# A third matrix product for 17 steps in place of a VectorE sum, and four gathers spread over four steps, in a Fourier-mixing and gated-convolution kernel

## The chip, the cores and the metric

The kernel runs on one core of a Trainium2 chip. The metric is the device time of one execution in microseconds (us). A core has five engines with a queue of instructions each: TensorE (in the profile PE, and PEld for its weight loads), VectorE (DVE), ScalarE (ACT), GpSimd (POOL) and SyncE (SP), which here only issues transfers. Each engine works its queue in the order in which the program issues; between engines there are semaphores. SBUF is the working memory, PSUM the memory that TensorE writes its products to.

## The reference

Per batch (8), a sequence of 3136 rows with 256 features is transformed by a two-dimensional Fourier transform, of which the real part is kept. Then follow a matrix product to 1024 features, a ReLU, a convolution with three taps along the sequence (one weight per tap and feature), a gate (the value times its sigmoid) and a matrix product back to 256 features. All numbers are float32.

```python
X = np.fft.fft(np.fft.fft(x, axis=1), axis=2).real
h = np.maximum(X @ w_in, 0.0)
conv_out = sum(conv_w[k] * hp[:, k:k + S, :] for k in range(3))   # hp: h with a zero row on both ends
out = (h * sigmoid(conv_out)) @ w_out
```

## The kernel before, in words

**The transform.** For each batch, x is loaded in two halves: one plain transfer by SP and four gathers by indirect DMA on GpSimd (`mirrored`, L131), which bring rows in mirrored order. VectorE folds the halves by sums and differences (`fold_ops`, L151 to L194; 14 operations per batch), TensorE multiplies the folded rows by tables of cosines and sines (`units`, tile `pd`), and VectorE combines these into two tiles per batch, `pt` and `qt` (`PQ`), of 128 features by 1569 frequencies. The transform along the features is merged into the weight: `G` holds two products of `w_in` with cosines and sines. One feature of the spectrum is handled apart (`Feature`, tile `ft`), and arrives as a row `eb`.

**The steps.** The main part works in 256 steps (batch, chunk, feature block): 8 batches, 4 chunks of the frequencies (some 386 columns each), 8 blocks of 128 of the 1024 features. Because x is real, the frequencies k and S-k come from the same two products: with `pa` = seed + G0 pt and `pb` = G1 qt, row k of h is relu(pa + pb), row S-k is relu(pa - pb). So one step makes a front half and a back half of a row tile `h` of 770 or 832 columns.

The code issues everything by hand, in the order of a loop over turns t (`LAG` is 3), in which each engine's queue receives:

- ScalarE: the sigmoids of step t-2 (L725, two instructions); the two copies of `pb` of step t+1 into `nb`, as pb and as -pb (`copies`, L693); the seed of step t+2 into `pa` (`seed`, L672: feature row times weight); the first tap of step t (`first_tap`, L707); at the end of a chunk six copies of finished outputs (L752).
- TensorE: the two products of step t+1 (`products`: `pb`, then `pa`); then `mm2` of step t-3 (12 instructions into `po`, accumulated over the eight feature blocks); then parts of the transform of the next batch.
- VectorE: the two sums of step t (`combine`, L702: `TENSOR_ADD_SAT` adds `pa` and one half of `nb`, clips below at 0 and writes a half of `h`, the back half in reverse order); the second tap of step t-1 (L712); a fold, or part of the conversion of the weights from 64-bit floats (L543 to L561, in turns 0, 2, 3, 5 and 7); the third tap of step t-1 (L712); the gate of step t-2 for its first 385 columns or so (L733).
- GpSimd: in chunk 0 a small memset of the two end columns of `h` (`row_of`, L678, called at the head of `combine`); the gate of step t-2 for the other columns (L732, L735); the gathers.

The lists of extra work are filled by `at(turn, where, fn)`: "first" stands behind the sigmoids, "act" behind the copies, "dve" between the taps, "pool" and "load" behind the gate, "pe" at the end. For batch 1, folds stand in turns 9 to 19 (the first half of x in turns 9 to 13, the second from turn 14 on), the products of its transform from turn 20 on. `feat.place` (POOL, VectorE, ACT) stands in turn 5, its stages in turns 14 to 18.

Buffers: `pa` has two, `pb` one, `nb` two, `h` four, `g` five. Waits between engines are derived from which instruction reads and writes which tile.

Of the kernel before, what the change touches and what calls it, by code (L numbers as in the profile page):

```python
# [12 lines left out]
AF = mybir.ActivationFunctionType  # L13
# [19 lines left out]
BIG = 3.4028234663852886e38  # L33
# [3 lines left out]
def kernel(  # L37
# [10 lines left out]
    nc = tc.nc  # L48
    B, S, D = x.shape
    F = moe_w_in.shape[1]  # L50
    P = 128
# [9 lines left out]
    NF = F // P  # L61
# [27 lines left out]
    act = nc.scalar.activation  # L89

    def mm(o, l, r, start, stop):
        nc.tensor.matmul(o, l, r, start=start, stop=stop, skip_group_check=True)  # L92
# [16 lines left out]
    def load_ops(b, h, eng, other=None, held=False):  # L109


        def plain():
            t = xp.tile([P, 8, 2, D], F32, name="xh", tag="xh")
            xh[b, h] = t
            if held:

                nc.gpsimd.memset(t[0:1, 0, 0, 0:1], 0.0)
            eng.dma_start(out=t[0:NP, 0:4], in_=bass.AP(
                tensor=x.tensor, offset=x.offset + (b * S + 1 + 2 * h) * D,
                ap=[[HQ * D, NP], [Q4 * D, 4], [1, 2 * D]]))  # L120

        def zero():
            t = xh[b, h]
            for s0, n, r in ((0, 4, 0), (4, 3, 1), (7, 1, 0)):
                (other or eng).dma_start(out=t[NP:KR, s0:s0 + n], in_=bass.AP(
                    tensor=x.tensor, offset=x.offset + (b * S + r * Q4) * D,
                    ap=[[D, 1], [Q4 * D, n], [0, 2], [1, D]]))

        def mirrored(m):
            def f():  # L130
                nc.gpsimd.indirect_dma_start(  # L131
                    out=xh[b, h][0:NP, 7 - m].rearrange("p q d -> p (q d)"),
                    out_offset=None,
                    in_=bass.AP(tensor=x.tensor, offset=x.offset,
                                ap=[[2 * D, B * S // 2], [1, 2 * D]]),
                    in_offset=bass.IndirectOffsetOnAxis(ap=idx[0:NP, 0:1], axis=0),
                    element_offset=(b * S + (4 - m) * Q4 - HO + 2 * (1 - h)) * D)
            return f
        return [plain] + [zero] * h + [mirrored(m) for m in range(4)]
# [73 lines left out]
    PQ, eb, er = {}, {}, {}  # L213
# [416 lines left out]
    G = const.tile([P, 2, F], F32, name="G")  # L630
# [29 lines left out]
    hs, gs, pa, pb, po, nb = {}, {}, {}, {}, {}, {}  # L660

    def cut(s):
        b, c, f = s
        ch = chunks[c]
        return ch, ch.k1 - ch.k0, slice(f * P, (f + 1) * P)

    def seed(s):
# [3 lines left out]
        pa[s] = psa.tile([P, 512], F32, name="pa", tag="pa")  # L671
        act(pa[s][:, 0:n], eb[b, c], AF.Copy, scale=ge[:, f:f + 1])  # L672

    def row_of(s):
        hs[s] = hp.tile([P, HW], F32, name="h", tag="h")
        w = chunks[s[1]].w
        if chunks[s[1]].zeros:
            nc.gpsimd.memset(hs[s][:, 0:w:w - 1], 0.0)  # L678

    def products(s):  # L680
        b, c, f = s
        ch, n, fs = cut(s)
        pb[s] = psb.tile([P, 512], F32, name="pb", tag="pb")
        mm(pb[s][:, 0:n], G[0:P - 1, 1, fs], PQ[b][1][0:P - 1, ch.k0:ch.k1], True, True)
        mm(pa[s][:, 0:n], G[:, 0, fs], PQ[b][0][:, ch.k0:ch.k1], False, True)

    def copies(s):

        ch, n, fs = cut(s)
        p = pb.pop(s)  # L690
        nb[s] = nbp.tile([P, 2, HN], F32, name="nb", tag="nb")
        for i, cols in enumerate((ch.fcols, ch.cols)):
            act(nb[s][:, i, cols], p[:, cols], AF.Copy, scale=-1.0 if i else 1.0)  # L693

    def combine(s):

        ch, n, fs = cut(s)
        a, c = pa.pop(s), nb.pop(s)
        row_of(s)
        h = hs[s]  # L700
        for i, (to, cols) in enumerate(((h[:, ch.front], ch.fcols), (h[:, ch.back][:, ::-1], ch.cols))):
            nc.vector._custom_dve(TENSOR_ADD_SAT, out=to, in0=a[:, cols], in1=c[:, i, cols], s0=BIG, s1=0.0)  # L702

    def first_tap(s):
        n = chunks[s[1]].w - 2
# [99 lines left out]
    n = chunks[0].k1  # L805
    p = psd.tile([P, 512], F32, name="pd", tag="pd")
# [12 lines left out]
    def at(cycle, where, fn):  # L819
        side.setdefault((cycle, where), []).append(fn)  # L820
# [11 lines left out]
    for cycle, c in ((2, 0), (3, 2), (5, 4), (7, 6)):  # L832
        shared(cycle, w_out, c)
    for j, fn in enumerate(load_ops(1, 1, nc.sync)):
        at(NF + 1 + j // 3, "load", fn)

# [22 lines left out]
    for b in range(1, B):  # L861
        begin, us, *_ = units(b)
        us = us[0:4] + us[5:]
        c0, n = ends[b], per * b - 3 - ends[b]
# [12 lines left out]
    for b in range(1, B):  # L877
        ops, singles = fold_ops(b)
        c0, n = ends[b - 1], ends[b] - ends[b - 1]
# [14 lines left out]
    n = len(steps)  # L894
    seed(steps[0])
    seed(steps[1])
    products(steps[0])
    copies(steps[0])
    column(1)
    for t in range(n + LAG):  # L900
        def run(where):
            for fn in side.get((t, where), []):
                fn()
        if 0 <= t - 2 < n:
            sigmoid(steps[t - 2])
        run("first")
        if t + 1 < n:
            products(steps[t + 1])
            copies(steps[t + 1])
        run("act")  # L910
        if t < n:
            combine(steps[t])
        if t + 2 < n:
            seed(steps[t + 2])
        if t < n:
            first_tap(steps[t])

        if 0 <= t - 1 < n:
            tap(steps[t - 1], 1)
        run("dve")  # L920
        if 0 <= t - 1 < n:
            tap(steps[t - 1], 2)
        if 0 <= t - 2 < n:
            gate(steps[t - 2])
        run("pool")
        run("load")
        if t >= LAG:
            mm2(steps[t - LAG])
        run("pe")
# [66 lines left out]
```

## Time and profile before

| | |
|---|---|
| median of 10 runs | 1196.52 us (1193.44 to 1198.23) |
| the profiled execution | 1195.56 us |
| its span, first to last instruction | 1193.6 us |
| TensorE busy | 1156.1 us, 97% of the span, 4802 matmuls |
| VectorE busy | 1134.5 us, 95% |
| ScalarE busy | 879.0 us, 74% |
| GpSimd busy | 476.8 us, 40% |
| mean granted TensorE clock | 0.996 of full speed |

The busy time of an engine is the sum of its instructions' times; a busy time per window, a timeline of one engine and a list of what ended each idle time are taken from the same execution. A row of a timeline gives the start in us from the span's start, the length, the engine, the line of the kernel, the operation, what it writes and reads, and how many instructions are merged (x2); the rows of merged instructions overlap the next by a little, so the distance from one start to the next is what an instruction costs its queue. A clock of 1.00 is full speed.

Turn 0 begins at about 46 us. The table of steps that the prediction uses, by the start of VectorE's sums (L702): step 3 at 62.22, step 6 at 78.63, step 10 at 97.10, step 12 at 105.97, step 13 at 113.39, step 20 at 148.05 us.

### The profile page before, as it was taken

How to read it: one execution, taken by the hardware profiler on the slowest of the kernel's cores; microseconds unless marked ns; L12 is line 12 of the kernel's file. 1: busy time of each engine (PE TensorE's matmuls, PEld its weight loads, DVE VectorE, ACT ScalarE, POOL GpSimd, SP SyncE). 2: the span in 40 equal slices, each digit the busy share in tenths (PEclk: the TensorE clock that was granted, in tenths of full speed). 3: DMA queues.
4: the chain of work that ended last, by engine and by line, in shares of the span. 5: the costliest groups of instructions: out<-in, count | busy, mean ns of one | idle time of the engine just before them, and what ended most of it. 6: DMA issues, size and time to landing. Idle time of an engine off the chain costs nothing.

```text
span 1193.6 us, 15307 instructions
## 1 busy us (share of the span) xinstructions
PE 1156.1 (97%) x4802; PEld 889.1 (74%) x4802; DVE 1134.5 (95%) x1642; ACT 879.0 (74%) x1824; POOL 476.8 (40%) x540
## 2 busy tenths in 40 slices
PE   4978999999999999999999999999999999999998
PEld 2756677678777777777777777777777777777776
DVE  7899999999999999999999999999998998999996
ACT  2577667677777777777777777787776777788884
POOL 5225636454273333624345243632224232442224
PEclk9999999999999999999999999999999999999999
DMA  9802243212031210202021020310001100110000
GB/s 226 193 18 81 72 57 101 62 54 71 10 95 45 68 41 24 85 27 81 27 88 52 20 62 27 96 40 27 27 23 32 32 27 27 47 34 28 27 27 31
DMA packets 70067, 66.07 MB, mean 55 GB/s; under 512 B 28107, under 2 KB 57683, under 8 KB 69987
## 3 DMA queue, kind: packets, MB, share of 16 engines
q1 hardware_dynamic: 64349, 51.98, 15.4%
q0 software_dynamic: 5120, 12.85, 3.9%
q8 instruction: 38, 0.62, 0.2%
q14 instruction: 42, 0.34, 0.1%
q10 hardware_dynamic: 518, 0.28, 0.1%
HBM read 39.33 MB, written 25.74 MB: 55 GB/s over the span
## 4 chain that ended last, share of the span: by engine, by line
PE 87%; DVE 4%; issue 3%; POOL 3%; ACT 2%; DMA 0%; ACTq 0%; POOLq 0%; DVEq 0%; SPq 0%
PE po L92 53%; PE pb L92 14%; PE pa L92 13%; PE pd L92 7%; DVE g L712 2%; POOL xh L131 1%; DVE h L702 1%; ACT nb L693 0%; ACT os L752 0%; DVE g L733 0%; ACT g L725 0%; POOL left L735 0%; POOL g L732 0%; ACT pa L672 0%; DMA er<-qt 0%
## 5 line engine op out<-in xcount | busy, mean ns | idle before, releaser
L92 PE MATMUL po<-wout,g 128*128 128x256 f32 x3072 | 708.4, 380 | 15.7 <-DVE g L733 15.5
L92 PEld LDWEIGHTS po<-wout,g 128*128 128x128 f32 x3072 | 581.6, 190 | 162.9 <-DVE g L733 29.2
L712 DVE SCALAR_TENSOR_TENSOR g<-h,cw,g 128x770 f32<-128x770 f32 (+1 forms) x512 | 580.3, 1133 | 6.2 <-ACT g L707 2.2
L732 POOL TENSOR_TENSOR g<-g,h 128x385 f32<-128x385 f32 (+1 forms) x256 | 276.1, 1079 | 670.3 <-ACT g L725 468.3
L693 ACT ACTIVATE nb<-pb 128x386 f32<-128x386 f32 (+3 forms) x512 | 227.5, 498 | 183.7 <-PE pb L92 183.1
L725 ACT ACTIVATE g<-g 128x385 f32<-128x385 f32 (+2 forms) x512 | 244.4, 529 | 81.8 <-DVE g L712 78.5
L702 DVE CUSTOM_DVE_ANT_0 h<-pa,nb 128x386 f32<-128x386 f32 (+3 forms) x512 | 264.2, 556 | 6.5 <-POOL h L678 6.5
L707 ACT ACTIVATE g<-h,cw 128x770 f32<-128x770 f32 (+1 forms) x256 | 244.0, 953 | 0.0
L92 PE MATMUL pb<-qt,G 127*128 127x387 f32 (+2 forms) x512 | 213.8, 498 | 0.9 <-ACT G L641 0.9
L92 PE MATMUL pa<-pt,G 128*128 128x387 f32 (+2 forms) x512 | 211.8, 494 | 0.0
L672 ACT ACTIVATE pa<-eb,ge 128x387 f32<-128x387 f32 (+2 forms) x256 | 154.3, 603 | 2.5 <-DVE h L702 1.9
L92 PEld LDWEIGHTS pa<-pt,G 128*128 128x128 f32 x512 | 97.0, 189 | 73.5 <-issue 18.8
L733 DVE TENSOR_TENSOR g<-g,h 128x385 f32<-128x385 f32 (+1 forms) x256 | 147.5, 576 | 2.2 <-ACT g L725 2.2
L92 PE MATMUL pd<-tab,w 98*128 98x196 f32 (+3 forms) x448 | 118.4, 356 | 0.0
L131 POOL DMA_INDIRECT xh<-in_x_dram,idx x64 | 105.7, 1651 | 13.3 <-issue 10.6
L92 PEld LDWEIGHTS pb<-qt,G 127*128 127x128 f32 x512 | 91.0, 190 | 19.0 <-ACT G L641 1.8
L92 PEld LDWEIGHTS pd<-tab,w 98*128 98x128 f32 (+1 forms) x448 | 83.7, 191 | 12.3
L735 POOL TENSOR_TENSOR left<-g,h 128x64 f32<-128x64 f32 x64 | 63.8, 997 | 0.0
L752 ACT COPY os<-po 128x256 f32<-128x256 f32 x196 | 57.7, 392 | 8.1 <-PE po L92 4.7
L156 DVE TENSOR_TENSOR xh<-xh 98x1020 f32<-98x1020 f32 (+1 forms) x32 | 39.4, 1237 | 3.2 <-DMA xh<-in_x_dram,idx 3.2
L167 DVE TENSOR_TENSOR xh<-xh 98x1024 f32<-98x1024 f32 (+1 forms) x32 | 38.9, 1217 | 0.1
L178 POOL COPY w<-xh 98x4 f32<-98x4 f32 (+1 forms) x32 | 21.2, 662 | 7.3 <-DVE xh L172 3.7
(120 smaller groups left out, 315.3 us busy)
## 6 DMA issues: line engine op xcount, KB each, us to landing
out_dram<-os SPq DMA_DIRECT2D x192, 128.0 KB
xh<-in_x_dram SPq DMA_DIRECT2D x16, 784.0 KB
eb<-ed SPq DMA_DIRECT2D x16, 193.5 KB
tab<-dft_seq_dram SPq DMA_DIRECT2D x4, 589.5 KB
raw<-in_moe_w_in_dram SPq DMA_DIRECT2D x4, 512.0 KB
raw<-in_moe_w_out_dram SPq DMA_DIRECT2D x1, 2048.0 KB
eb<-ed SPq DMA_DIRECT2D x8, 209.0 KB
eb<-ed SPq DMA_DIRECT2D x7, 193.0 KB
```

Of the source, the lines that this page charges most:

```text
L92: nc.tensor.matmul(o, l, r, start=start, stop=stop, skip_group_check=True)
L131: nc.gpsimd.indirect_dma_start(out=xh[b, h][0:NP, 7 - m].rearrange("p q d -> p (q d)"), out_offset=None, in_=bass.AP(tensor=x.tensor, offs ...
L672: act(pa[s][:, 0:n], eb[b, c], AF.Copy, scale=ge[:, f:f + 1])
L693: act(nb[s][:, i, cols], p[:, cols], AF.Copy, scale=-1.0 if i else 1.0)
L702: nc.vector._custom_dve(TENSOR_ADD_SAT, out=to, in0=a[:, cols], in1=c[:, i, cols], s0=BIG, s1=0.0)
L707: act(gs[s], hs[s][:, 0:n], AF.Copy, scale=cw[:, 0, s[2]:s[2] + 1])
L712: stt(out=g, in0=h[:, k:k + n], scalar=cw[:, k, f:f + 1], in1=g, op0=ALU.mult, op1=ALU.add)
L725: act(gs[s][:, c], gs[s][:, c], AF.Sigmoid)
L732: gt(g[:, p], g[:, p], h[:, p], op=ALU.mult)
L733: vt(g[:, v], g[:, v], h[:, v], op=ALU.mult)
L735: gt(left[:, f, b % 2 * LEFT:(b % 2 + 1) * LEFT], g[:, r], h[:, r], op=ALU.mult)
L752: nc.scalar.copy(out=osb[:, j % 2], in_=pt[:, j % 2])
```

## The change

In steps 3 to 19 of batch 0 (`triple`), TensorE adds the `pb` product once more, into `pa`, so that `pa` becomes pa + pb. The front half of `h` is then made by ScalarE, as a Relu of `pa`; VectorE makes the back half alone, from `pa` - 2 pb, for which the single remaining copy of `pb` carries the factor -2. For these steps `row_of` is called in `copies`, one turn earlier than before. In all other steps nothing changes.

Of the six operations that load the second half of x of batch 1, the plain load, the zero rows and the first gather stay in turn 9; the other three gathers, which stood in turn 10 together, stand in turns 10, 11 and 12.

```diff
+    def triple(s):
+
+        return s[0] == 0 and 3 <= s[1] * NF + s[2] < 20
+
...
-        mm(pa[s][:, 0:n], G[:, 0, fs], PQ[b][0][:, ch.k0:ch.k1], False, True)
+        mm(pa[s][:, 0:n], G[:, 0, fs], PQ[b][0][:, ch.k0:ch.k1], False, not triple(s))
+        if triple(s):
+            mm(pa[s][:, 0:n], G[0:P - 1, 1, fs], PQ[b][1][0:P - 1, ch.k0:ch.k1], False, True)
...
-        for i, cols in enumerate((ch.fcols, ch.cols)):
-            act(nb[s][:, i, cols], p[:, cols], AF.Copy, scale=-1.0 if i else 1.0)
+        if triple(s):
+            act(nb[s][:, 1, ch.cols], p[:, ch.cols], AF.Copy, scale=-2.0)
+            row_of(s)
+            act(hs[s][:, ch.front], pa[s][:, ch.fcols], AF.Relu)
+        else:
+            for i, cols in enumerate((ch.fcols, ch.cols)):
+                act(nb[s][:, i, cols], p[:, cols], AF.Copy, scale=-1.0 if i else 1.0)
...
-        row_of(s)
+        if not triple(s):
+            row_of(s)
         h = hs[s]
         for i, (to, cols) in enumerate(((h[:, ch.front], ch.fcols), (h[:, ch.back][:, ::-1], ch.cols))):
-            nc.vector._custom_dve(TENSOR_ADD_SAT, out=to, in0=a[:, cols], in1=c[:, i, cols], s0=BIG, s1=0.0)
+            if i or not triple(s):
+                nc.vector._custom_dve(TENSOR_ADD_SAT, out=to, in0=a[:, cols], in1=c[:, i, cols],
+                                      s0=BIG, s1=0.0)
...
     for j, fn in enumerate(load_ops(1, 1, nc.sync)):
-        at(NF + 1 + j // 3, "load", fn)
+        at(NF + 1 + max(j - 2, 0), "load", fn)
```

## The prediction

> **What bounds the kernel now.** A step is one (batch, chunk, feature block), 256 in all; "turn t" is the pass of the step loop that adds up step t. TensorE's products of step t run in turn t-1, its output matmuls (`mm2`) of step t in turn t+3. I first read the page's busy line, which says only that two engines are near full:
>
> ```profile
> PE 1156.1 (97%) x4802; PEld 889.1 (74%) x4802; DVE 1134.5 (95%) x1642; ACT 879.0 (74%) x1824; POOL 476.8 (40%) x540
> ```
>
> So I read the table of busy times by stage next (columns: window, its length, then busy us of PE, PEld, DVE, ACT, POOL, granted clock, DMA share, GB/s). The change acts in turns 2 to 19, about 62 to 148 us; the third row is the stage behind it, the last one the steady state:
>
> ```profile
> 62.00:97.00 35.00, 28.59 (x112) 20.86 (x112) 33.49 (x54) 23.12 (x46) 8.98 (x19) 1.00 0.13 35
> 97.00:148.00 51.00, 45.14 (x174) 31.94 (x174) 50.93 (x72) 36.73 (x94) 30.59 (x23) 0.97 0.25 76
> 148.00:200.00 52.00, 51.82 (x223) 40.43 (x224) 51.19 (x80) 34.42 (x70) 24.75 (x27) 1.00 0.44 83
> 330.00:700.00 370.00, 370.00 (x1551) 289.03 (x1550) 359.85 (x524) 284.37 (x585) 157.70 (x176) 1.00 0.19 57
> ```
>
> Up to 148 us VectorE is full (33.49 of 35, 50.93 of 51) and TensorE is not; from 148 on TensorE is. The timelines show how the one waits for the other. VectorE in turn 10 (start, length; the number in brackets elsewhere is idle time):
>
> ```profile
> 97.10 1.02 DVE L702 CUSTOM_DVE_ANT_0 h<-pa,nb 128x386 f32<-128x386 f32 x2
> 98.04 1.01 DVE L712 SCALAR_TENSOR_TENSOR g<-h,cw,g 128x770 f32<-128x770 f32 x1
> 98.97 1.22 DVE L167 TENSOR_TENSOR xh<-xh 98x1024 f32<-98x1024 f32 x1
> 100.10 1.02 DVE L712 SCALAR_TENSOR_TENSOR g<-h,cw,g 128x770 f32<-128x770 f32 x1
> 101.03 0.55 DVE L733 TENSOR_TENSOR g<-g,h 128x385 f32<-128x385 f32 x1
> ```
>
> The two sums, the taps with a fold between them, the gate: each starts as the one before it ends. TensorE, four of the lines of the same stretch:
>
> ```profile
> 94.74 0.81 PE L92 MATMUL pb<-qt,G 127*128 127x387 f32 x2
> 95.40 0.81 PE L92 MATMUL pa<-pt,G 128*128 128x387 f32 x2
> 97.24 2.86 PE L92 MATMUL po<-wout,g 128*128 128x256 f32 x12 [1.03 <-DVE g L733]
> ...
> 113.53 4.46 PE L92 MATMUL po<-wout,g 128*128 128x256 f32 x12 [2.81 <-DVE g L733]
> ```
>
> `mm2` waits for the gate; behind the 2.81 us of idleness the clock row for 113.5 to 117.8 grants 0.61, and the block takes 4.30 us to the next product instead of 2.59. That too lies under VectorE now. The chain of waits says the same: between 60 and 113 us it runs mainly over DVE lines.
>
> **What the change takes off VectorE.** In 17 steps (3 to 19) one of two sums goes. From the first L702 (97.10) to the tap behind the pair (98.04) is 0.94 us, so one sum is 0.47: 17 x 0.47 = 8.0 us. VectorE's turns 3 to 19 run from 62.22 to 148.05, 85.8 us. One stall in them also goes: in turn 6 the sum waited 1.20 us for the memset of L678, queued on POOL behind `feat.place`; that memset is now issued one turn earlier, ahead of it. (Now step 7's memset stands behind `feat.place`: done at about 77.2, it holds the Relu of step 7, whose product ends at 76.3, for 0.9 us, on ScalarE, where the margin worked out below is 3.6.) Left: 85.8 - 8.0 - 1.2 = 76.6 us.
>
> **What it puts on TensorE.** The third product repeats the `pb` product into `pa`: by the starts above (94.74 to 95.40) it costs 0.655 us; bounds are this and 0.81, its own row, if it could not overlap its neighbour. Before: from `mm2` of step 0 (62.02) to that of step 17 (148.18) are 86.2 us. In them lie 17 blocks of `mm2` (2.59), 17 pairs of products (1.31) and the feature stage (2.0): 44.0 + 22.3 + 2.0 = 68.3, so 17.9 us are idle or slowed. The third products of steps 5 to 19 fall in here: 15 x 0.655 = 9.8. Those of steps 3 and 4 run before 62.02, 1.3 us, of which 0.7 fall in the gap from 61.33 to 62.02; 0.6 stay. TensorE without any idle time: 68.3 + 9.8 + 0.6 = 78.7 us. That exceeds VectorE's 76.6: **the bound passes to TensorE**, and the stage can shrink by 86.2 - 78.7 = 7.5 us at most.
>
> **Does it reach that?** I walked both queues through. TensorE would start `mm2` of step k at 62.64 + 4.56k; VectorE ends turn k+2, with the gate of step k, at 67.4, 70.7, 76.0, 79.3, 84.5, 87.4, 92.6, 96.5 for k = 1 to 8. TensorE comes to these at 67.2, 71.8, 76.3, 80.9, 85.4, 90.0, 94.6, 99.1. Only k = 1 (0.2 late) and k = 3 (nearly) make it wait: 0.3 us. Later the margin is 2 us and more, enough for the 1.7 us by which the tap at 106.90 was drawn out to 2.71 beside two POOL gates. In the steady state TensorE is busy 370.00 of 370 us beside a VectorE at 359.85, so a TensorE without gaps beside a nearly full VectorE exists in this kernel.
>
> **ScalarE: an instruction exchanged, a wait added.** The second copy of `pb` (two copies take 0.75 us of queue, one 0.37) becomes a Relu of `pa` of the same width: 0.37 to 0.55 (a sigmoid's row is 0.47); I take no change. L545 runs Relu between sigmoids without a table load, so none is added. But the Relu waits for the third product, 1.31 us behind `pb`, where the copy waited for `pb` alone: ScalarE stands up to 1.31 - 0.37 = 0.94 us. Behind it queue the seed of step t+2 (wanted by TensorE 2.59 + 0.65 us later; it takes 0.5) and the first tap of step t (wanted by VectorE in turn t+1). ScalarE idles 35.0 - 23.1 = 11.9 and 51.0 - 36.7 = 14.3 us here, 1.5 a turn, which covers it. From the third product over Relu, seed and first tap (2.0), tap to gate (3.5) and a further turn (4.6) to `mm2` are 10.1 us; TensorE asks for it after three turns, 13.7. Margin 3.6. The Relu also needs the `h` buffer (four of them) that the gate three steps back frees, on VectorE and on POOL.
>
> [...]
>
> **Gathers.** Turn 10 issues three gathers on POOL at once:
>
> ```profile
> 98.41 1.52 POOL L131 DMA_INDIRECT xh<-in_x_dram,idx  x1 [0.19 <-issue]
> 100.23 2.20 POOL L131 DMA_INDIRECT xh<-in_x_dram,idx  x1 [0.30 <-issue]
> 102.74 4.15 POOL L131 DMA_INDIRECT xh<-in_x_dram,idx  x1 [0.30 <-ACT nb L693]
> 106.92 0.88 POOL L732 TENSOR_TENSOR g<-g,h 128x385 f32<-128x385 f32 x1
> ```
>
> The gate at 106.92 could have run at about 102 (its sigmoid ends at 102.2). Now it would hold the Relu of step 13 through the `h` buffer, and `mm2`; one gather a turn (1.5 to 4.2 us against a turn of 4.56) lets each gate through. Nothing is late: the last is issued in turn 12, lands some 4 us later (median of `xh`) and is read in turn 15. SP's load is not moved. By itself this is worth 0 (TensorE waited 0.18 for it) to 1.7 us (the drawn-out tap); as TensorE is the bound after, I count 0.
>
> **Sum.** 7.5 - 0.3, less 0.5 for POOL hand-offs like the one above: 6.7 us (bounds: with 0.81 for the third product 17 x 0.155 = 2.6 less, 4.1; nothing lost, 7.5). Behind 148 us TensorE has no gap to 200 (51.82 of 52), so the earlier start is passed on. VectorE's own lead is not: at 187.88 it waits for ScalarE even now. The profiled execution, 1195.56 (span 1193.6 and 2.0 around it), would be 1188.9; it lies 0.96 under the median of 1196.52, so the median becomes **1189.8**.
>
> **Rivals.** (a) TensorE keeps part of its gaps. For: it waited 12.5 us for VectorE's gates in this stage, and POOL's gates were drawn out to 3.55 and 4.24 us beside VectorE's taps. If 3.5 us remain: 3.2 gained, 1193.3. (b) More: a lead that VectorE keeps beyond 200 us could fill the 2.8 us that TensorE idles between 200 and 232: 9.5 gained, 1187.0. Against: the wait at 187.88. (c) The gain is waited away behind 148 us, by data that come no earlier: 1196.5. Against: VectorE's only wait there is that one of 0.61 us. (d) **Slower.** The sum comes right behind its products: before, it could start 0.75 us after `pb` (two copies), now 1.31 + 0.47 = 1.78. A step bound by this pays 1.03 - 0.47 = 0.56, any other saves 0.42; it loses from 8 of 17 steps on, and all 17 give +9.5: 1206.0. For: the chain does pass ScalarE's `nb` copies at 97.69 and 102.25. Against: VectorE's queue is full, and its sum follows `pb` by 3.8 us or more from turn 10 to 19. That the third product is not issued can be excluded: TensorE's order shows it in each of the 17 steps.
>
> **Numbers.** Forecast 0.55 (1188.2 to 1191.5), (a) 0.20, (b) 0.10, (c) 0.07, (d) 0.08. A run of this kernel tells 0.2%, 2.4 us, from no change: faster (under 1194.1) is 0.55 + 0.10 + 0.19 = 0.84, same 0.08, slower 0.08. The range takes in (a) and (b) and leaves out (c) and (d): 1187.0 to 1194.0.
>
> **What would show it.** TensorE without gaps from about 67 to 141 us, each turn 4.5 to 4.6 us, no grant of 0.61; the first `pd` matmuls of batch 1 some 7 us earlier (150.88 before); VectorE with idle time, ended by ScalarE, in the later turns; POOL gates of turns 11 and 12 a turn apart. Wrong: idle time before `mm2` still ended by L733's successor, or ScalarE idle behind PE in most turns with VectorE waiting for it, which is (d).

## The result, and the profile after

| | before | after |
|---|---|---|
| median of the runs | 1196.48 us (28 runs, 1193.44 to 1198.23) | 1192.80 us (8 runs, 1189.88 to 1193.43) |
| profiled execution (span) | 1195.56 (1193.6) us | 1190.91 (1189.1) us |
| start of `mm2` of step 0 to that of step 17, "the stage" below | 62.02 to 148.18: 86.16 us | 61.47 to 143.32: 81.85 us |

The changed kernel takes 0.9963 of the time before, 95% interval [0.9955, 0.9972]: 4.4 us gained by the ratio, 3.7 by the medians, 4.31 in the stage, where 6.7 were forecast. The time lies in the range. The changed kernel's times fall into two groups, 1189.9 to 1190.3 us and 1192.8 to 1193.4, at mean granted clocks of 0.999 and of 0.997 to 0.998: the median belongs to the second, while the profiled execution (0.999) lies near the first. The start-up moves the start of `mm2` of step 0 between 60.6 and 64.0 us from one profiled execution to another, so kernels are compared below by the ratio and by the length of the stage.

The busy line and the table by stage of the changed kernel (columns as before: window, its length, busy us of PE, PEld, DVE, ACT, POOL, granted clock, DMA share, GB/s). The first two rows are the stage, split at 97 us, the third the stage behind it, the fourth the whole stage, the last the steady state:

```profile
PE 1162.4 (98%) x4836; PEld 893.8 (75%) x4836; DVE 1131.2 (95%) x1625; ACT 879.4 (74%) x1824; POOL 478.6 (40%) x540
```

```profile
61.15:97.00 35.85, 35.25 (x141) 26.28 (x140) 35.54 (x51) 26.36 (x53) 12.26 (x21) 1.00 0.13 34
97.00:143.20 46.20, 44.66 (x178) 31.54 (x177) 46.13 (x59) 33.55 (x87) 29.64 (x21) 1.00 0.28 83
143.20:195.00 51.80, 51.80 (x223) 40.34 (x223) 50.99 (x80) 34.35 (x70) 24.69 (x27) 1.00 0.45 83
61.47:143.32 81.85, 79.71 (x317) 57.64 (x316) 81.47 (x108) 59.71 (x139) 41.71 (x41) 1.00 0.21 62
330.00:700.00 370.00, 369.91 (x1549) 288.73 (x1549) 359.29 (x523) 282.81 (x578) 157.61 (x178) 1.00 0.18 56
```

TensorE is nearly full now, as forecast: 79.71 of 81.85 us, at clock 1.00 throughout. But so is VectorE, 81.47 of 81.85, although it was to have shed 8.0 us of sums: in the stage of the kernel before it was busy for 84.58 us, only 3.1 more. Where the 8.0 us went is seen in single instructions. VectorE in turns 10 and 11 (start, length):

```profile
93.91 0.55 DVE L715 CUSTOM_DVE_ANT_0 h<-pa,nb 128x386 f32<-128x386 f32 x1
94.38 1.47 DVE L726 SCALAR_TENSOR_TENSOR g<-h,cw,g 128x770 f32<-128x770 f32 x1
95.78 1.21 DVE L167 TENSOR_TENSOR xh<-xh 98x1024 f32<-98x1024 f32 x1
96.91 1.01 DVE L726 SCALAR_TENSOR_TENSOR g<-h,cw,g 128x770 f32<-128x770 f32 x1
97.84 0.55 DVE L747 TENSOR_TENSOR g<-g,h 128x385 f32<-128x385 f32 x1
98.31 0.55 DVE L715 CUSTOM_DVE_ANT_0 h<-pa,nb 128x386 f32<-128x386 f32 x1
98.78 1.00 DVE L726 SCALAR_TENSOR_TENSOR g<-h,cw,g 128x770 f32<-128x770 f32 x1
```

One sum per turn is left, as intended. The tap right behind it took 1.47 us at 94.38; the same form later in that turn, at 96.91, took 1.01. GpSimd (POOL) beside them, with the idle time before each in brackets:

```profile
94.17 0.86 POOL L746 TENSOR_TENSOR g<-g,h 128x385 f32<-128x385 f32 x1 [3.01 <-ACT g L739]
95.22 1.51 POOL L131 DMA_INDIRECT xh<-in_x_dram,idx  x1 [0.19 <-issue]
98.80 4.32 POOL L746 TENSOR_TENSOR g<-g,h 128x385 f32<-128x385 f32 x1 [2.07 <-issue]
```

POOL's gate starts at 94.17, 0.26 us after the sum, and runs to 95.03. The sum ends its turn on VectorE at 94.38; 94.38 + 1.47 - 1.01 = 94.84, so the tap made no headway for some 0.5 us, about the time that the gate still had. In the next turn it is the other way round: the tap at 98.78 took its 1.00, and the gate beside it was drawn out from 0.86 to 4.32 us. Of the 17 gates in the stage three were drawn out to 3 us and more, as that one was; beside each of the other 14 a row of VectorE was drawn out, 13 times a tap and once L172. Before the change POOL's gate of turn 10 was this:

```profile
97.36 0.86 POOL L732 TENSOR_TENSOR g<-g,h 128x385 f32<-128x385 f32 x1 [3.02 <-ACT g L725]
```

It ended at 98.22, so all but its last 0.2 us lay beside the two sums that the prediction shows from 97.10, and the tap behind them (98.04) took 1.01. So the two sums together had been the cover of POOL's gate, and one is too short for it. None of this is idle time: the row of the instruction that stands is longer, and the engine counts as busy.

### The profile page after: what moved, and what is told of

Same layout as the page of the kernel before. It is cut to its first block, busy times and chain, and to the rows that moved or that the text cites. A ratio compares the mean times of both kernels' runs of the same rounds, so it can differ in the third digit from the quotient of the medians.

```text
span 1189.1 us, 15341 instructions
## 1 busy us (share of the span) xinstructions
PE 1162.4 (98%) x4836; PEld 893.8 (75%) x4836; DVE 1131.2 (95%) x1625; ACT 879.4 (74%) x1824; POOL 478.6 (40%) x540
## 4 chain that ended last, share of the span: by engine, by line
PE 83%; DVE 8%; ACT 2%; issue 2%; POOL 1%; DMA 0%; ACTq 0%; DVEq 0%; POOLq 0%; SPq 0%
PE po L92 51%; PE pb L92 13%; PE pa L92 13%; PE pd L92 7%; DVE g L726 3%; DVE h L715 1%; DVE g L747 1%; POOL xh L131 1%; DMA out_dram<-os 0%; ACT os L766 0%; ACT nb L704 0%; DVE xh L167 0%; POOL left L749 0%; DVE xh L156 0%; ACT g L739 0%
## 5 line engine op out<-in xcount | busy, mean ns | idle before, releaser
L726 DVE SCALAR_TENSOR_TENSOR g<-h,cw,g 128x770 f32<-128x770 f32 (+1 forms) x512 | 583.8, 1140 | 6.2 <-ACT g L721 2.2
L746 POOL TENSOR_TENSOR g<-g,h 128x385 f32<-128x385 f32 (+1 forms) x256 | 279.1, 1091 | 655.5 <-ACT g L739 464.1
L704 ACT ACTIVATE nb<-pb 128x386 f32<-128x386 f32 (+2 forms) x478 | 212.9, 500 | 180.7 <-PE pb L92 180.1
L715 DVE CUSTOM_DVE_ANT_0 h<-pa,nb 128x386 f32<-128x386 f32 (+2 forms) x495 | 256.3, 556 | 5.0 <-POOL h L682 4.5
L747 DVE TENSOR_TENSOR g<-g,h 128x385 f32<-128x385 f32 (+1 forms) x256 | 148.0, 578 | 3.8 <-ACT g L739 3.8
L156 DVE TENSOR_TENSOR xh<-xh 98x1020 f32<-98x1020 f32 (+1 forms) x32 | 39.5, 1238 | 3.3 <-DMA xh<-in_x_dram,idx 3.3
```

Of the source, the lines that this page charges most:

```text
L726: stt(out=g, in0=h[:, k:k + n], scalar=cw[:, k, f:f + 1], in1=g, op0=ALU.mult, op1=ALU.add)
L746: gt(g[:, p], g[:, p], h[:, p], op=ALU.mult)
L747: vt(g[:, v], g[:, v], h[:, v], op=ALU.mult)
```

## The experiments

Three theories were set against each other. **P** ("port" in the texts below, the author's picture, which no run tests): a VectorE instruction that takes its inputs from SBUF, as the tap takes `h` and `g`, and a GpSimd instruction that reads SBUF do not run at once (the tap at 94.38, 1.47 us for 1.01); the sum, which reads `pa` in PSUM, does run beside it (before, the pair at 97.10 cost 0.94 us beside a gate of 0.86, and the pair at 101.50, with no gate beside it, 0.94 too). **H**, the hand-offs of rival (a): gates come late through the queues of ScalarE and GpSimd. **W**: any GpSimd instruction beside the tap draws it out. Stage lengths were 86.16 us before and 81.85 after.

**One part of the change alone.** `e1_gathers_only` is the kernel before with the spread gathers; `e2_third_only` is the changed kernel with the gathers as they were:

```diff
-        at(NF + 1 + j // 3, "load", fn)
+        at(NF + 1 + max(j - 2, 0), "load", fn)
```

(e1; in e2 the reverse.)

> Theory P (port): a VectorE tap, which reads two tiles of SBUF, stands still while a GpSimd gate that reads SBUF runs. With both sums kept (0.94 us a turn), a gate of 0.87 us lies beside them, so only the collision at 106.9 us (1.7 us) can go: 0 to 1.7 us faster, 1194.8 to 1196.5. Theory H (hand-offs: TensorE waits for gates that come late through ScalarE and GpSimd queues): the late gates of turns 11 and 12 come on time, but VectorE stays the bound: about 0.

> Third products alone, with the three gathers of turn 10 left together. P: the taps are drawn out as in the changed kernel (some 0.5 us in most turns), and the gathers hold POOL's gates of turns 11 and 12 back, now also the Relu of step 13: 2.0 to 3.7 us faster than before, 1192.8 to 1194.5. H: the late gates cost as much as they delay the Relu, some 4 us in one place: 0 to 1 us faster, 1195.5 to 1196.5.

e1: ratio 0.9989 [0.998, 0.9998], stage 84.67. e2: 0.997 [0.9958, 0.9982], stage 82.14. The gathers alone are worth 1.3 us by the medians (1195.02 against 1196.31), inside the 0 to 1.7 that was given; on top of the third product only 0.3 us of the stage, which the runs cannot tell from nothing. e2's median, 1192.68, is 0.1 under the 1192.8 to 1194.5 that P gave, and far from H's 1195.5 or more. With three gathers in a turn, `mm2` of step 10 waited 1.81 us in e2; spread, TensorE's longest wait in the stage is 0.84. The 2 to 3 us missing from the forecast are not with the gathers.

**GpSimd's gate left out**, in steps 1 to 17, from the kernel before (e3) and from the changed one (e4):

```diff
-        gt(g[:, p], g[:, p], h[:, p], op=ALU.mult)
+        if not (s[0] == 0 and 1 <= s[1] * NF + s[2] < 18):
+            gt(g[:, p], g[:, p], h[:, p], op=ALU.mult)
```

> The kernel before, in which GpSimd's gate multiplication of steps 1 to 17 is left out (the turns of the change; the columns stay ungated). P: only the three drawn-out taps of this stage go, 1.7 + 0.8 + 0.6: about 3 us faster, 1193.5. H: TensorE waited 0.2 us for these gates: 0 to 0.5 us faster, 1196.

> The changed kernel, with GpSimd's gate multiplication of steps 1 to 17 left out in the same way. P: every tap takes 1.0 us again, VectorE's turns 3 to 19 shrink from 82.0 to about 74 us, TensorE becomes the bound without gaps (about 78.5 us from the output matmuls of step 0 to those of step 17): 3 to 4 us faster than the changed kernel, 1189 to 1190, and 4 to 5 us faster than e3. H: the waits behind VectorE's gates and ScalarE remain; within 0.5 us of the changed kernel, 1192.5, and 3.5 us faster than e3.

e3: 0.9975 [0.9965, 0.9986], median 1193.08, stage 82.92. e4: 0.9945 [0.9931, 0.9959], median 1189.92, stage 79.00. Both are where P put them, and against H. That the two differ by "4 to 5 us" was too much: 3.2 by the medians, 3.9 in the stage. The reason is in e4's row of the table by stage:

```profile
63.65:142.65 79.00, 78.67 (x318) 58.30 (x317) 74.83 (x110) 60.27 (x139) 20.67 (x27) 1.00 0.23 65
```

PE is busy 78.67 of 79.00 us, and VectorE, 74.83, has 4.2 to spare: the bound has passed to TensorE, which is the stage that the prediction had for the changed kernel itself (78.7 and 0.3). VectorE now shows idle time that ScalarE ends, without the stage being longer for it:

```profile
101.67 0.55 DVE L715 CUSTOM_DVE_ANT_0 h<-pa,nb 128x386 f32<-128x386 f32 x1
103.69 1.02 DVE L726 SCALAR_TENSOR_TENSOR g<-h,cw,g 128x770 f32<-128x770 f32 x1 [1.47 <-ACT g L721]
```

e4 also takes work from GpSimd's queue, so it does not yet tell reading from being there at all. That is the next one.

**GpSimd writes the same columns but reads nothing** (e5, the changed kernel):

```diff
-        gt(g[:, p], g[:, p], h[:, p], op=ALU.mult)
+        if s[0] == 0 and 1 <= s[1] * NF + s[2] < 18:
+            nc.gpsimd.memset(g[:, p], 0.5)
+        else:
+            gt(g[:, p], g[:, p], h[:, p], op=ALU.mult)
```

> The changed kernel, in which GpSimd's gate multiplication of steps 1 to 17 is replaced by a memset of the same columns (0.5; a part of the gate is left out): GpSimd stays in the same place of its queue and writes SBUF, but reads none. P (a tap that reads two tiles stands still while GpSimd reads SBUF): the taps take 1.0 us, the stage from the output matmuls of step 0 to those of step 17 takes about 79 us as in e4, total 1189.5 to 1190.5. Rival W (any GpSimd instruction that touches SBUF, or the rows of the page alone, draws the tap out): taps as in the changed kernel, stage about 82, 1192.5.

Ratio 0.994 [0.9925, 0.9954], median 1189.55, stage 79.02. A tap beside such a memset, in e5's timeline of both engines:

```profile
98.82 0.42 POOL L747 MEMSET g<- 128x385 f32 x1 [1.68 <-issue]
98.83 1.02 DVE L726 SCALAR_TENSOR_TENSOR g<-h,cw,g 128x770 f32<-128x770 f32 x1
```

It started with the memset and took no longer than any other; the longest tap of e5 took 1.023 us, from 60 to 143. GpSimd's memset of 0.42 us at the same place, which reads nothing, draws out no tap, which is against W.

**GpSimd's gate doubled** (e8): behind it, a second multiplication, of 384 of the same columns, into a scratch tile.

```diff
         gt(g[:, p], g[:, p], h[:, p], op=ALU.mult)
+        if s[0] == 0 and 1 <= s[1] * NF + s[2] < 18:
+            q = slice(p.start, p.start + 3 * P)
+            gt(left[:, 0:3].rearrange("p f i -> p (f i)"), g[:, q], h[:, q], op=ALU.mult)
```

> The changed kernel with the suspected cost doubled: in steps 1 to 17 GpSimd multiplies the same columns a second time, into a scratch tile (a further 0.87 us of reading a turn; nothing waits for the result). P: VectorE's two-input instructions stand still for most of it: 5 to 14 us slower than the changed kernel, 1198 to 1207. H: GpSimd is busy 41.9 of 82 us here, so it has the time: 0 to 1 us slower, 1192.5 to 1193.5.

Ratio 1.0076 [1.0061, 1.0092], median 1205.63, 12.8 us over the changed kernel; stage 94.60, VectorE busy 94.22 of it. One turn of e8, VectorE and POOL:

```profile
94.61 0.55 DVE L715 CUSTOM_DVE_ANT_0 h<-pa,nb 128x386 f32<-128x386 f32 x1
94.85 0.87 POOL L746 TENSOR_TENSOR g<-g,h 128x385 f32<-128x385 f32 x1 [1.46 <-ACT g L739]
95.07 1.46 DVE L726 SCALAR_TENSOR_TENSOR g<-h,cw,g 128x770 f32<-128x770 f32 x1
95.80 1.46 POOL L749 TENSOR_TENSOR left<-g,h 128x384 f32<-128x384 f32 x1
96.46 3.00 DVE L156 TENSOR_TENSOR xh<-xh 98x1020 f32<-98x1020 f32 x2
```

The tap stands for the first multiplication, the second for the tap (1.46 us, started at 95.80 while the tap ran to 96.46), and the two L156, 1.2 us each elsewhere and 2.3 together, take 3.00. L156 reads `xh` alone and GpSimd `g` and `h`, so what they wait for is not a shared tile. A GpSimd multiplication that takes 0.87 us undisturbed, added in each of 17 turns, 14.8 us in all, cost 12.8: beside this VectorE queue most of GpSimd's added reading time is paid for.

**A smaller share for GpSimd** (e6 after, e7 before): the whole computation, with the division of the gate moved so that POOL's part is 208 columns instead of 385 in steps 1 to 17, and VectorE's 562.

```diff
-        return slice(0, n // 2), slice(n // 2, n), slice(n, w)
+        m = n - 208 if s[0] == 0 and 1 <= s[1] * NF + s[2] < 18 else n // 2
+        return slice(0, m), slice(m, n), slice(n, w)
```

> The changed kernel with a smaller GpSimd share of the gate in steps 1 to 17: 208 of some 770 columns instead of 385, the rest on VectorE (0.47 us to about 0.68); the whole computation is done. P: GpSimd's gate (0.87 to about 0.5 us) now fits beside the one sum, 8 us of drawn-out taps shrink to 1 or 2, against 17 x 0.21 = 3.6 us more gate on VectorE: VectorE's turns 3 to 19 take 78 to 79.5 us, the bound is near TensorE's 79: 1.5 to 3 us faster than the changed kernel, 1189.8 to 1191.2. H (hand-offs) and W (drawn out by any GpSimd instruction): VectorE only gets more to do: 2 to 3.6 us slower than the changed kernel, 1194.5 to 1196.

> The kernel before with the same smaller GpSimd share in steps 1 to 17; the whole computation is done. P: two sums already cover the gate, so only the rare collisions can go (3 us at most), and VectorE gets 3.6 us more: 0.5 to 3.6 us slower than before, 1197 to 1200. If it were as fast as e6, the smaller share and not its meeting with the third product would be the cause.

e6: ratio 0.994 [0.9925, 0.9956], median 1189.49, stage 79.21: faster than both kernels, and 0.3 us faster than P's range. e7: 1.0008 [0.9999, 1.0017], median 1197.48, stage 87.47: no gain, and by the interval no certain loss. One turn of e6:

```profile
93.70 0.73 DVE L748 TENSOR_TENSOR g<-g,h 128x562 f32<-128x562 f32 x1
94.35 0.55 DVE L715 CUSTOM_DVE_ANT_0 h<-pa,nb 128x386 f32<-128x386 f32 x1
94.82 1.01 DVE L726 SCALAR_TENSOR_TENSOR g<-h,cw,g 128x770 f32<-128x770 f32 x1
95.75 1.21 DVE L167 TENSOR_TENSOR xh<-xh 98x1024 f32<-98x1024 f32 x1
```

```profile
94.28 0.57 POOL L747 TENSOR_TENSOR g<-g,h 128x208 f32<-128x208 f32 x1 [2.87 <-PE pb L92]
95.03 4.40 POOL L131 DMA_INDIRECT xh<-in_x_dram,idx  x1 [0.18 <-issue]
```

POOL's gate of 0.57 us now ends with the one sum (94.85 against 94.82), and the tap takes 1.01. VectorE pays 0.73 - 0.55 = 0.18 us a turn for the larger share and saves the 0.46 by which the tap stood. The smaller share gains nothing where two sums still cover the gate (e7): there VectorE pays the 0.18 us a turn for nothing. It is not the share, but the share against the cover.

## Why the prediction was right or wrong

The sign, the range and the third product's price were right; the likeliest size was not.

**The step that failed** is the margin that kept GpSimd out of the sum: "Later the margin is 2 us and more, enough for the 1.7 us by which the tap at 106.90 was drawn out to 2.71 beside two POOL gates." It took that row for one mishap. It was the rule where the two met, and the change made them meet in nearly every turn. So the term "76.6 us" for VectorE's turns 3 to 19 was mis-sized: they ran from 61.17 to 143.18, 82.0 us. Summed rows of the two kernels in these turns close the account:

| VectorE, turns 3 to 19 | before | after |
|---|---|---|
| sums (L702; L715) | 17.3 | 9.3 |
| taps (L712; L726), 34 each | 37.0 | 41.4 |
| the fold's last line, L172 | 1.4 | 2.4 |
| idle (window less busy) | 1.6 | 0.4 |

The sums gave their 8.0 us, and the stall at L678 its 1.2. The taps took back 4.4 (from 1.09 us each to 1.22; with no gate on GpSimd, e4, 1.01) and L172, beside a gate at 106.00, another 1.0: 9.2 - 5.4 = 3.8, which is 85.8 to 82.0. Part of this was there before, which is why e3 gains as well: without the gate its 34 taps took 34.4 us instead of 37.0, and the fold line L193 0.69 instead of 1.24 in turn 16, together the 3.2 us by which its stage is shorter.

Side by side, taps took at most 1.023 us with GpSimd's memset beside them (e5), 1.47 beside its gate (94.38), and 1.01 behind two sums that had the gate beside them (98.04, before). What in the two engines makes the one stand for the other is not shown.

The other steps:

- **The third product**: right. With VectorE out of the way (e4) the stage is 79.00 where 78.7 + 0.3 were worked out, so 0.655 us each holds.
- **"The bound passes to TensorE"**: wrong for the changed kernel, where VectorE stays full, 81.47 of 81.85; right for e4, e5 and e6. The idle time on VectorE ended by ScalarE, which was to show it, came in e4 and e5, not in the changed kernel.
- **TensorE's waits**: the one at k = 1 came, 0.60 us for 0.2 foreseen. Three more came that were not foreseen: 0.84 at 108.89, 0.39 at 114.09, 0.30 at 139.32, all ended by VectorE's gate, L747, the successor of L733: the prediction's own sign of being wrong, though in four waits of 2.1 us together, where there were 12.8 before. The grant of 0.61 is gone: the clock is 1.00 over the stage, against 0.98 before.
- **ScalarE**: right. The Relu waited 1.2 us for gates of POOL, in two places, but VectorE never waits for the Relu in the stage; in e4, with a quicker VectorE, the sum waited for a Relu once, 0.41 us: it started at 131.02, as the Relu (130.50, 0.49 us) ended. No table load was added: the last is at 55.21, of 1.28 us, ahead of the stage, as it was before (56.27).
- **Behind the stage**: right. TensorE is busy 51.80 of 51.80, and the waits of before at 201.06, 205.75, 211.19, 216.77 and 230.88 come back, equally long within 0.01 us, 4.87 us earlier. The first `pd` matmuls of batch 1 start 4.9 us earlier, where about 7 were expected, so (b) and (c) both fall.
- **POOL's gates of turns 11 and 12 a turn apart**: not so; the one at 98.80 ran to 103.12, and the next began at 106.00, behind a gather, in a turn that began at 102.31.
- **Rival (a)** has the time, 1193.3, but only half the mechanism: gates of POOL drawn out beside VectorE's taps were named for it, but the time was lost mainly on the other side, in taps that stand for the gates. **Rival (d)** never showed: the sum does not wait for its products. That it stands behind the Relu, which the 1.78 us of (d) take in, is seen once, in e4's sum at 131.02.

What is not settled is what decides which of the two stands. The gates at 94.17 and at 124.00 both begin some 0.2 us ahead of the tap (94.38; 124.22); beside the first the tap stood (1.47), beside the second the gate did (3.08, the tap 1.00). So the order of the recorded starts does not decide it. One execution of each kernel was traced, so whether the same instruction stands in every execution is not shown.

## What to carry to other kernels

Before an instruction is taken off a full engine, ask what ran beside it on the other engines that could not have run beside its successor: here the sums from PSUM were where GpSimd's gate cost nothing (0.94 us the pair, 1.01 the tap behind it). Standing still in this way is recorded as busy time, so compare the lengths of rows of the same form (1.01 against 1.47), not idle time. And when the cover shrinks, shrink what it covers: 208 columns instead of 385 brought the stage from 81.85 to 79.21 us.

## What the runs showed of the hardware that was not expected

- The two sides pay unevenly: a tap that stands loses about the rest of the gate (0.5 us), a gate that stands was held for 2 to 3.5 us (4.32 at 98.80, 3.08 at 124.00, 3.76 at 140.22, for 0.86), across several VectorE instructions (behind 98.80 two taps, L193, L194 and VectorE's gate); GpSimd's next row starts only then (103.06 behind the first). No wait of TensorE or VectorE in the stage was ended by a GpSimd gate, and GpSimd was busy 41.71 us of 81.85.
- Two taps, at 109.22 and 130.02, took 2.22 and 2.24 us, 1.2 more than their own time and more than a whole gate, though they began 0.5 us ahead of it. Each began while GpSimd was issuing a gather, and the gate followed that at once. A gather alone did not draw a tap out: in the kernel before, the taps at 104.56 and 132.55 lay wholly beside gathers (from 102.74, 4.15 us; from 132.31, 2.62 us) and took 1.02 and 1.01. Why the taps at 109.22 and 130.02 stood before the gate's row began stays open.
- Issuing an indirect gather took GpSimd 0.99 us at 100.59 in e5 and 4.40 at 95.03 in e6. Whether VectorE's rows beside them draw these out was not tried.
